# Three moves in a fused attention, mixing and FFN kernel: tile 2's weights, unit passes, the first block's centring

## The chip, the cores and the metric

The kernel runs on one core of one Trainium2 chip. The metric is the device time of one execution in microseconds (us); smaller is better. TensorE (PE) multiplies matrices into PSUM, VectorE (DVE), ScalarE (ACT) and GpSimd (POOL) work on tiles in SBUF, and SyncE (SP) issues most DMAs. Each engine runs its instructions in the order in which they are written; between engines there are semaphores. TensorE's clock has two levels here, 1.2 and 2.4 GHz; the profile gives the granted clock of a stretch as a share of the higher one.

## The reference

Three stages follow one another on 4 batches of 768 tokens with 384 channels. The first is a recurrent attention; the change leaves its arithmetic alone. Then:

```python
# mixing of tokens (x: [4, 768, 384])
theta = x @ w_theta
zr, zi = x * cos(theta), x * sin(theta)
y = einsum('ts,bsd->btd', w_tok_r, zr) + einsum('ts,bsd->btd', w_tok_i, zi)
u = x + y
x = u + max(u @ w_ch, 0)                 # "channel product"
# feed-forward network (FFN)
mu, var = mean(x), mean((x - mu) ** 2)   # over the channels
xn = (x - mu) / sqrt(var + 1e-6) * g_ln
out = x + max(xn @ w_ch1, 0) @ w_ch2     # 384 -> 1536 -> 384
```

All weights arrive as 64-bit numbers. Each product is made of three: a value is split into a rounded high part and the rest (names ending in h and l, or hi and lo), and high times high, low times high and high times low are added up in PSUM.

## The kernel before

**Attention** runs 24 chunks and takes about the first 229 us. `late(c, k)`, called in slot k of chunk c, puts the beginnings of the next stage into it.

**Mixing** is a loop over the 24 pairs of MIX: batch b and block s of 128 source tokens. The first 12 steps take blocks 0 to 2 of each batch, the rest blocks 3 to 5. Step i multiplies z of block i with the mixing weights of token tile s: `mix(i, 0)` and `mix(i, 1)`, 18 matmuls each. Between the halves come a channel product if one is due, then the angles of step i + 2: `theta` (9 matmuls of x with w_theta), `angles` (kk on ScalarE, nf on VectorE), `sines` and `cosines` (ScalarE), and the transposes and copies of x for the step after that (pt, xh, xl, u). At the start of step i, `turn(i + 1)` multiplies x with the sines and cosines (zf on VectorE) and rounds it (zh on ScalarE), and `rest(i + 1)` subtracts (zl on VectorE). So zl of a step is made while the step before it is multiplied. PSUM tiles pc, pth, pt and pst share two buffers under the tag "pa".

**Weights.** The class Weights handles the 64-bit weights in units, one behind the other in the order in which they were queued. A unit is loaded (raw; two staging buffers), its magnitude is taken (ScalarE, line 765; in attention's slots VectorE, line 761, and the clamps at once), it is clamped (VectorE, lines 771 and 772), assembled (VectorE, lines 781 and 782) into one of three buffers t, and split into hi (ScalarE, line 795) and lo (POOL or VectorE, line 802). `step()` does a piece of this in each late slot of attention. `pump()` does it in the loop: it finishes the unit before the last one, assembles the last one and begins the next. PA[i] pumps stand between turn and rest of step i; PB[i] pumps behind the angles, where only the clamps are done ahead of the channel product. The units are w_theta, the mixing weights w0 to w5 (w(s,q): tile s, half q), FFN weights that are multiplied with g on POOL and stored as 32-bit numbers in DRAM (`stash`, tile flat), and w_ch. At last the FFN weights f0 to f3 are loaded back from flat and split.

**The first FFN block's preparation** is the list of `pre(0)`: split of u, three channel products, the sum of u over the channels on VectorE (`total`), the mean subtracted and the rest split (`centre`: a product with ones into pst, then three rounds of subtraction, rounding and subtraction), the squares (ScalarE) and their sum (POOL, `total` again), and `rstd`: again a product with ones, then square root, reciprocal and one step of refinement on VectorE, ScalarE and POOL. The loop places these pieces in steps 15 to 23.

**FFN.** From 441.9 us on, 8 blocks of 12 features' tiles run on a TensorE that hardly pauses: `up` (9 matmuls into ph; hh on ScalarE, hl on VectorE), and two tiles later `down` (9 matmuls into acc).

The lines that the change touches move: line 795 becomes 797, 802 becomes 804, and from line 848 on six are added, so that zl's line 916 is 922 and the channel product's addition 992 is 998.

Of the kernel before, what the change touches and what calls it, by code (L numbers as in the profile page):

```python
# [7 lines left out]
F32R = mybir.dt.float32r  # L8
# [654 lines left out]
C = 384  # L663
# [9 lines left out]
class Weights:  # L673
# [110 lines left out]
    def parts(self, u, raw, t, clamped):  # L784
        nc = self.nc
        self.ready.add(u[0])
        if len(u) == 5:
            dst, g = u[3:]
            w = t[:, 0].rearrange("p (k c) -> p k c", k=KB)
            nc.gpsimd.tensor_tensor(out=w, in0=w, in1=bc(g.unsqueeze(2), [128, KB, 128]), op=ALU.mult)  # L790
            self.stores.append((dst, t))
            return lambda: None
        hi, lo, scale, split = u[3:]
        if scale is None:
            nc.scalar.copy(out=hi, in_=t)
            n = t.shape[1]
            split = n if split is None else split

            def low():
                for e, r in ((nc.gpsimd, slice(0, split)), (nc.vector, slice(split, n))):  # L800
                    if r.stop > r.start:
                        e.tensor_tensor(out=lo[:, r], in0=t[:, r], in1=hi[:, r].bitcast(F32), op=ALU.subtract)
        else:
            nc.scalar.activation(out=hi, in_=t, func=AF.Copy, scale=scale)

            def low():
                nc.vector.scalar_tensor_tensor(out=lo, in0=t, scalar=scale, in1=hi.bitcast(F32), op0=ALU.mult, op1=ALU.subtract)
        return low


class Mixer:
# [21 lines left out]
    def load_w(self, s, wtok, pool, wts, w=None):  # L833
        w = self.W[s] = w or [pool.tile([128, 4, C], F32R, name=f"w{s}_{i}") for i in range(2)]
        for q in range(2):
            wts.add(("w", s, q), wtok[s, q], w[0][:, 2 * q:2 * q + 2], w[1][:, 2 * q:2 * q + 2], split=0 if s > 1 else None)

# [265 lines left out]
def build(tc, a):  # L1103
# [8 lines left out]
    with tc.manual_schedule(), outer:  # L1112
# [14 lines left out]
        def late(c, k):  # L1127
# [11 lines left out]
            if (c, k) == (19, 2):  # L1139
                mx.open(ph1, tc)  # L1140
                for s in range(2):
                    mx.load_w(s, a["wtok"], mx.cst, wts)
                wts.load()
# [35 lines left out]
        for s in (2, 3, 4, 5):  # L1179
            mx.load_w(s, a["wtok"], None, wts, [slot(f"w{s}_{i}", 2 * (s - 2) + i, [128, 4, C], F32R) for i in range(2)])  # L1180
        spare = ExitStack()
# [11 lines left out]
        def two_f(f, hi, lo):  # L1193
            for n in range(2):
                ff.load_f(f + n, flat, hi[:, 2 * n:2 * n + 2], lo[:, 2 * n:2 * n + 2], wts)

        SLOTS = {"uh": 2, "ul": 3, "xh": 6, "xl": 7}
        soon = {"uh": 0, "ul": 1}
# [8 lines left out]
        n = len(MIX)  # L1207
        PA = [3] + [1] * 21 + [2] * 2
        PB = [0] * 18 + [1] * 4 + [2] * 2
        wp = Late()  # L1210
# [3 lines left out]
        for i in range(n):  # L1214
            b, s = MIX[i]
            assert ("w", s, 1) in wts.ready
            if i + 1 < n:
                mx.turn(i + 1)
            for _ in range(PA[i]):
                wts.pump()  # L1220
            if i + 1 < n:
                mx.rest(i + 1)
            mx.mix(i, 0, yp)
            for _ in range(PB[i]):
                wts.clamps()
            for k in {16: (1,), 17: (2,), 18: (3,)}.get(i, ()):
                todo[k]()
# [16 lines left out]
            if i == 7:  # L1244
                spare.close()
                ff.load_ch(a["wch"], outer.enter_context(tc.tile_pool(name="wch", bufs=1)), wts)
                stash(range(6, NF))
            if i == 17:
                two_f(0, *[slot(f"f0_{k}", k, [128, 4, C], F32R) for k in range(2)])
            if i == 22:  # L1250
                two_f(2, *[slot(f"f2_{k}", 4 + k, [128, 4, C], F32R) for k in range(2)])
            assert i < 15 or ("c", 2) in wts.ready, wts.todo
            if i == 15:
                wp.pool = ff.sp = Spare(mx.cst, ("w1_0", "w1_1"))
            for k in {15: (0,), 20: (4,), 21: (5,), 22: (6,), 23: (7,)}.get(i, ()):
                todo[k]()
# [64 lines left out]
```

## Time and profile before

| | us |
|---|---|
| median of 3 runs | 791.89 (790.45 to 794.86) |
| profiled execution, own time | 792.09 |
| span in the trace | 790.3 |
| TensorE busy | 709.3 (90%) |
| VectorE busy | 518.8 (66%) |
| ScalarE busy | 356.7 (45%) |
| POOL busy | 212.2 (27%) |
| mean granted TensorE clock | 0.968 |

Times in the rows below count from the start of the span. A row of the time-ordered view has the start, the duration, the engine, the line, what it writes and reads, and in brackets the engine's idle time just ahead of it with what ended that time.

### The profile page before, as it was taken

The page shows a single profiled execution, that of the slowest core. Times are in us where ns is not written, and L with a number is a line of the kernel's source. Part 1 is how long each engine was busy: PE and PEld are TensorE (multiplying, and loading weights), DVE is VectorE, ACT ScalarE, POOL GpSimd, SP SyncE. Part 2 cuts the span into 40 slices and gives each one's busy share as a digit, 9 for nine tenths or more (in the row PEclk, how much of TensorE's full clock was granted, in tenths as well). Part 3 has the DMA queues.
Part 4 walks back from the last instruction along what each step waited for, and adds up shares of the span by engine and source line. Part 5 has one row for each costly group of instructions (what it writes and reads, how often), then busy time and mean ns, then how long its engine had stood idle before and what let it go on. Part 6 is the DMA issues. An engine that isn't in the chain of part 4 may idle for free.

```text
span 790.3 us, 19137 instructions
## 1 busy us (share of the span) xinstructions
PE 709.3 (90%) x8059; PEld 654.2 (83%) x8062; DVE 518.8 (66%) x868; ACT 356.7 (45%) x782; POOL 212.2 (27%) x232
## 2 busy tenths in 40 slices
PE   4588788777686999999999899999999999999997
PEld 2455555544466999999999899999999999999997
DVE  5889989986858888889886555435353444444342
ACT  1267776787765776555444334122223222131210
POOL 4755655743110001202120332313121112112120
PEclk7799999999998999999999999999999999999999
DMA  8767766324434223542350130000000000000000
GB/s 265 232 178 209 196 194 185 117 89 133 155 134 170 80 76 105 148 133 80 120 179 22 60 100 1 31 1 31 1 31 1 30 1 31 1 1 31 1 31 30
DMA packets 29717, 71.41 MB, mean 90 GB/s; under 512 B 4928, under 2 KB 17472, under 8 KB 29632
## 3 DMA queue, kind: packets, MB, share of 16 engines
q1 hardware_dynamic: 29632, 70.19, 28.5%
q8 instruction: 63, 1.03, 0.6%
q14 instruction: 22, 0.18, 0.1%
HBM read 56.02 MB, written 9.44 MB: 83 GB/s over the span
## 4 chain that ended last, share of the span: by engine, by line
PE 68%; DVE 16%; ACT 7%; issue 3%; DMA 3%; POOL 2%; SPq 1%; ACTq 0%; DVEq 0%; POOLq 0%
PE acc L1068 19%; PE ph L1049 19%; PE y L935 14%; PE pc L990 4%; PE pth L875 3%; ACT bdw L439 3%; DVE prod L356 3%; PE S L447 2%; DVE XT L365 1%; PE py L473 1%; DMA raw<-wtok 1%; PE RW L435 1%; DVE t L781 1%; DVE u L944 1%; DVE Ti L365 1%
## 5 line engine op out<-in xcount | busy, mean ns | idle before, releaser
L935 PE MATMUL y<-w,zh 128*128 128x384 f32 x576 | 154.1, 341 | 1.8 <-ACT zh L910 1.3
L1068 PE MATMUL acc<-hh,f 128*128 128x384 f32 x576 | 147.2, 336 | 0.0
L1054 DVE SCALAR_TENSOR_TENSOR hl<-ph,hh 128x384 fp32r<-128x384 f32 x96 | 52.3, 553 | 112.7 <-ACT hh L1053 112.7
L1053 ACT ACTIVATE hh<-ph 128x384 fp32r<-128x384 f32 x96 | 46.7, 491 | 162.9 <-PE ph L1049 162.9
L1049 PE MATMUL ph<-xh,f 128*128 128x384 f32 x576 | 117.2, 338 | 0.0
L935 PEld LDWEIGHTS y<-w,zh 128*128 128x128 f32 x576 | 105.4, 189 | 2.4 <-ACT zh L910 1.6
L935 PE MATMUL y<-w,zl 128*128 128x384 f32 x288 | 98.3, 341 | 8.1 <-DVE zl L916 8.1
L1068 PEld LDWEIGHTS acc<-hh,f 128*128 128x128 f32 x576 | 104.5, 188 | 0.0
L1049 PEld LDWEIGHTS ph<-xh,f 128*128 128x128 f32 x576 | 102.8, 189 | 0.0
L1068 PE MATMUL acc<-hl,f 128*128 128x384 f32 x288 | 97.2, 337 | 2.4 <-DVE hl L1054 2.4
L1049 PE MATMUL ph<-xl,f 128*128 128x384 f32 x288 | 66.0, 337 | 0.0
L439 ACT COPY bdw<-RW 32x192 f32<-32x192 f32 x192 | 59.6, 310 | 10.7 <-PE RW L435 8.1
L935 PEld LDWEIGHTS y<-w,zl 128*128 128x128 f32 x288 | 55.0, 191 | 8.7 <-DVE zl L916 8.7
L1068 PEld LDWEIGHTS acc<-hl,f 128*128 128x128 f32 x288 | 54.2, 188 | 2.7 <-DVE hl L1054 2.7
L452 ACT COPY bds<-S 48x384 f32<-48x384 f32 x92 | 43.5, 473 | 28.3 <-PE S L447 26.9
L447 PE MATMUL S<-bdw,ktt 128*48 128x192 f32 x368 | 42.0, 352 | 15.3 <-ACT bdw L439 15.1
L790 POOL TENSOR_TENSOR t<-t,g 128x384 f32<-128x384 f32 x12 | 16.9, 1411 | 137.9 <-DVE t L782 134.8
L1049 PEld LDWEIGHTS ph<-xl,f 128*128 128x128 f32 x288 | 52.0, 189 | 0.0
L435 PEld LDWEIGHTS RW<-Rs,pt 32*32 32x32 f32 x1472 | 19.5, 108 | 31.8 <-DVE Rs L427 24.4
L447 PEld LDWEIGHTS S<-bdw,ktt 128*48 128x48 f32 x368 | 20.7, 128 | 29.9 <-ACT bdw L439 23.8
L1078 POOL TENSOR_TENSOR o<-u,o 128x384 f32<-128x384 f32 x21 | 20.8, 1017 | 85.0 <-DVE o L1077 85.0
L435 PE MATMUL RW<-Rs,pt 32*32 32x48 f32 x1472 | 25.8, 208 | 16.3 <-DVE Rs L427 16.2
(159 smaller groups left out, 1297.7 us busy)
## 6 DMA issues: line engine op xcount, KB each, us to landing
kqt<-kq SPq DMA_DIRECT2D x20, 512.0 KB, 5.9
raw<-wtok SPq DMA_DIRECT2D x12, 768.0 KB, 4.3
raw<-wff SPq DMA_DIRECT2D x12, 768.0 KB, 4.9
bdk<-kq SPq DMA_DIRECT2D x40, 192.0 KB, 4.2
vt<-vin SPq DMA_DIRECT2D x24, 192.0 KB, 4.8
ktt<-ktok SPq DMA_DIRECT2D x24, 192.0 KB, 4.0
x<-ys SPq DMA_DIRECT2D x96, 48.0 KB, 2.6
flat<-t SPq DMA_DIRECT2D x12, 384.0 KB, 5.5
```

Source lines behind the costliest of these rows:

```text
L356: eng.tensor_tensor(out=pr[:, j], in0=bc(lhs[:, j].unsqueeze(2), [128, i, c, kk]), in1=bc(rhs[:, j].unsqueeze(1), [128, i, c, kk]), op=ALU ...
L435: nc.tensor.matmul(RW[h][rr, 1, j, :], PT[c // 4][rr, m0 + j, :], Rs[rr, j, :], start=True, stop=True)
L439: nc.scalar.copy(out=b[rr, :, r, :], in_=RW[h][rr, 1, :, :])
L447: nc.tensor.matmul(S_ps[h][64 * e:64 * e + D, g, :], KT[c][:, 2 * h + g, e, :], b[:, 2 * g + e, :, :], start=(c == 0 and g == 0), stop=Tru ...
L452: nc.scalar.copy(out=n[ee, :, e, :], in_=S_ps[h][ee, :, :].rearrange("p g (r d) -> p (g r) d", r=4))
L875: nc.tensor.matmul(ps, l[:, k], self.tw[w][:, k], start=(n == 0), stop=(n == 8))
L935: nc.tensor.matmul(self.Y[q], l[:, ri, 128 * k:128 * k + 128], self.W[s][w][:, 2 * ri + h], start=(first and w == ri == 0 and l is zh), st ...
L990: nc.tensor.matmul(ps, self.wc[w][:, k, 128 * e:128 * e + 128], r[:, k], start=(n == 0), stop=(n == 8))
L1049: nc.tensor.matmul(ps, w[:, 0, 128 * k:128 * k + 128], r[:, k], start=(n == 0), stop=(n == 8))
L1053: nc.scalar.activation(out=hh, in_=ps, func=AF.Relu)
L1054: nc.vector.scalar_tensor_tensor(out=hl, in0=ps, scalar=0.0, in1=hh.bitcast(F32), op0=ALU.max, op1=ALU.subtract)
L1068: nc.tensor.matmul(self.ACC[j][e], w[:, 1, 128 * e:128 * e + 128], r, start=(f == 0 and n == 0), stop=(f == NF - 1 and n == 2))
```

## The change

1. `load_w` may be given its target tiles later, and the units of token tile 2 are queued together with those of tiles 0 and 1, in slot (19, 2) of attention. The DMA of w(2,0) is issued some 13 us earlier, and its magnitude and clamps are done by VectorE in attention's last slot; the DMA of w(2,1) goes ahead of the last chunk's stores of x.
2. In step 0, rest(1) stands straight behind turn(1), ahead of the pumps, which are two instead of three.
3. In steps 16 to 18 the pump moves from PA to PB, that is behind the channel product and the angles; steps 19 to 21 have their one pump in PA alone.
4. The sum of u is placed in step 18 (before: 20), the centring in 19 (21), the squares in 20 (22) and rstd in the middle of 22 (the end of 23). The centred tiles xh and xl take buffer slots 0 and 1 (before: 6 and 7).
5. f0 and f1 are queued in step 21 (before: 17), for slots 6 and 7.

```diff
@@ parts, load_w
+        if callable(hi):
+            hi, lo = hi(), lo()
...
     def load_w(self, s, wtok, pool, wts, w=None):
-        w = self.W[s] = w or [pool.tile([128, 4, C], F32R, name=f"w{s}_{i}") for i in range(2)]
+        if pool:
+            w = [pool.tile([128, 4, C], F32R, name=f"w{s}_{i}") for i in range(2)]
+        self.W[s] = w
         for q in range(2):
-            wts.add(("w", s, q), wtok[s, q], w[0][:, 2 * q:2 * q + 2], w[1][:, 2 * q:2 * q + 2], split=0 if s > 1 else None)
+            r = slice(2 * q, 2 * q + 2)
+            wts.add(("w", s, q), wtok[s, q], lambda r=r: self.W[s][0][:, r], lambda r=r: self.W[s][1][:, r],
+                    split=0 if s > 1 else None)
@@ late, slot (19, 2)
-                for s in range(2):
-                    mx.load_w(s, a["wtok"], mx.cst, wts)
+                for s in range(3):
+                    mx.load_w(s, a["wtok"], mx.cst if s < 2 else None, wts)
@@ before the loop
         for s in (2, 3, 4, 5):
...
+            if s > 2:
+                mx.load_w(s, a["wtok"], None, wts, w)
+            mx.W[s] = w
...
-        SLOTS = {"uh": 2, "ul": 3, "xh": 6, "xl": 7}
+        SLOTS = {"uh": 2, "ul": 3, "xh": 0, "xl": 1}
...
-        PA = [3] + [1] * 21 + [2] * 2
-        PB = [0] * 18 + [1] * 4 + [2] * 2
+        PA = [2] + [1] * 15 + [0] * 3 + [1] * 5
+        PB = [0] * 16 + [1] * 3 + [0] * 3 + [1] * 2
@@ the loop
             if i + 1 < n:
                 mx.turn(i + 1)
+            if i == 0:
+                mx.rest(1)
             for _ in range(PA[i]):
                 wts.pump()
-            if i + 1 < n:
+            if 0 < i < n - 1:
                 mx.rest(i + 1)
...
-            for k in {16: (1,), 17: (2,), 18: (3,)}.get(i, ()):
+            for k in {16: (1,), 17: (2,), 18: (3,), 22: (7,)}.get(i, ()):
...
-            if i == 17:
-                two_f(0, *[slot(f"f0_{k}", k, [128, 4, C], F32R) for k in range(2)])
+            if i == 21:
+                two_f(0, *[slot(f"f0_{k}", 6 + k, [128, 4, C], F32R) for k in range(2)])
...
-            for k in {15: (0,), 20: (4,), 21: (5,), 22: (6,), 23: (7,)}.get(i, ()):
+            for k in {15: (0,), 18: (4,), 19: (5,), 20: (6,)}.get(i, ()):
```

How the order of VectorE's instructions changes is seen at three places. A row has the source line, the operation, what it writes and reads, and the size; x_70 is the block of x that becomes z of step 1.

VectorE at the end of attention and in step 0, before:

```order
L861 TENSOR_TENSOR xl<-pt,xh 128x384
L909 TENSOR_TENSOR zf<-zf,x_70 128x768
L771 TENSOR_SCALAR t<-t 128x768
L772 TENSOR_SCALAR t<-t 128x768
L781 SCALAR_TENSOR_TENSOR t<-raw,t 128x768
L782 SCALAR_TENSOR_TENSOR t<-raw,t 128x768
L771 TENSOR_SCALAR t<-t 128x768
L772 TENSOR_SCALAR t<-t 128x768
L781 SCALAR_TENSOR_TENSOR t<-raw,t 128x768
L782 SCALAR_TENSOR_TENSOR t<-raw,t 128x768
L802 TENSOR_TENSOR w_1_4259<-t,w_0_4258 128x768
L916 TENSOR_TENSOR zl<-zf,zh 128x768
```

and after:

```order
L761 TENSOR_SCALAR t<-raw 128x768
L771 TENSOR_SCALAR t<-t 128x768
L772 TENSOR_SCALAR t<-t 128x768
L867 TENSOR_TENSOR xl<-pt,xh 128x384
L915 TENSOR_TENSOR zf<-zf,x_70 128x768
L922 TENSOR_TENSOR zl<-zf,zh 128x768
L781 SCALAR_TENSOR_TENSOR t<-raw,t 128x768
L782 SCALAR_TENSOR_TENSOR t<-raw,t 128x768
L771 TENSOR_SCALAR t<-t 128x768
L772 TENSOR_SCALAR t<-t 128x768
L781 SCALAR_TENSOR_TENSOR t<-raw,t 128x768
L782 SCALAR_TENSOR_TENSOR t<-raw,t 128x768
```

zl, which stood behind two whole units, now follows zf, and the magnitude and clamps of a unit have come to stand ahead of xl.

VectorE in steps 16 and 17, before; u_65 is the block that the channel products are added to:

```order
L909 TENSOR_TENSOR zf<-zf,x_2922 128x768
L771 TENSOR_SCALAR t<-t 128x768
L772 TENSOR_SCALAR t<-t 128x768
L781 SCALAR_TENSOR_TENSOR t<-raw,t 128x768
L782 SCALAR_TENSOR_TENSOR t<-raw,t 128x768
L916 TENSOR_TENSOR zl<-zf,zh 128x768
L992 SCALAR_TENSOR_TENSOR u_65<-pc,u_65 128x384
L885 SCALAR_TENSOR_TENSOR nf<-kk,pth 128x384
L865 TENSOR_TENSOR u_4250<-u_4250,pt 128x3x128
L861 TENSOR_TENSOR xl<-pt,xh 128x384
L909 TENSOR_TENSOR zf<-zf,x_72 128x768
```

and after:

```order
L915 TENSOR_TENSOR zf<-zf,x_2922 128x768
L922 TENSOR_TENSOR zl<-zf,zh 128x768
L771 TENSOR_SCALAR t<-t 128x768
L772 TENSOR_SCALAR t<-t 128x768
L998 SCALAR_TENSOR_TENSOR u_65<-pc,u_65 128x384
L891 SCALAR_TENSOR_TENSOR nf<-kk,pth 128x384
L871 TENSOR_TENSOR u_4258<-u_4258,pt 128x3x128
L867 TENSOR_TENSOR xl<-pt,xh 128x384
L781 SCALAR_TENSOR_TENSOR t<-raw,t 128x768
L782 SCALAR_TENSOR_TENSOR t<-raw,t 128x768
L915 TENSOR_TENSOR zf<-zf,x_72 128x768
```

Ahead of each addition into u_65 (line 992, now 998) stood four passes of a unit; now its two clamps stand there, and the other two passes come behind xl.

VectorE from step 22 to the FFN's first block, before; w_0 and w_1 in the rows of lines 1002 to 1036 hold the sums, f_1 is the low part of FFN weights:

```order
L909 TENSOR_TENSOR zf<-zf,x_72 128x768
L916 TENSOR_TENSOR zl<-zf,zh 128x768
L1002 TENSOR_TENSOR w_0_5626<-w_1_5627,w_0_5626 128x384
L944 TENSOR_TENSOR u_4251<-u_4251,y 128x384 x3
L802 TENSOR_TENSOR f_1_6211<-t,f_0_6210 128x384 x2
L944 TENSOR_TENSOR u_4251<-u_4251,y 128x384 x3
L1031 TENSOR_SCALAR w_1_5627<-pst 128x384
L1033 RECIPROCAL rs<-rs 128x384
L1034 SCALAR_TENSOR_TENSOR w_1_5627<-w_1_5627,rs 128x384
L1036 SCALAR_TENSOR_TENSOR rs<-w_1_5627,rs 128x384
L1054 SCALAR_TENSOR_TENSOR hl<-ph,hh 128x384 x3
```

and after, from step 21 on:

```order
L1008 TENSOR_TENSOR w_0_5626<-w_1_5627,w_0_5626 128x384
L915 TENSOR_TENSOR zf<-zf,x_2921 128x768
L922 TENSOR_TENSOR zl<-zf,zh 128x768
L891 SCALAR_TENSOR_TENSOR nf<-kk,pth 128x384
L915 TENSOR_TENSOR zf<-zf,x_72 128x768
L922 TENSOR_TENSOR zl<-zf,zh 128x768
L1037 TENSOR_SCALAR w_1_5627<-pst 128x384
L1039 RECIPROCAL rs<-rs 128x384
L1040 SCALAR_TENSOR_TENSOR w_1_5627<-w_1_5627,rs 128x384
L1042 SCALAR_TENSOR_TENSOR rs<-w_1_5627,rs 128x384
L804 TENSOR_TENSOR f_1_6164<-t,f_0_6163 128x384
L950 TENSOR_TENSOR u_4259<-u_4259,y 128x384 x3
```

The sum's subtraction (line 1002, now 1008) has come to stand ahead of zf and zl of steps 22 and 23, and the four rows of rstd (1031 to 1036, now 1037 to 1042) ahead of the subtractions for f0 to f3 instead of behind them.

## Rows read from the trace of the kernel before

**Rows 1.** The page's row of busy time, share and instructions, by engine.

```profile
PE 709.3 (90%) x8059; PEld 654.2 (83%) x8062; DVE 518.8 (66%) x868; ACT 356.7 (45%) x782; POOL 212.2 (27%) x232
```

**Rows 2.** PE's waits, 215 to 460 us: total, times, longest.

```profile
PE y L935 <- DVE zl L916: 8.1, 2, 7.5
...
PE pt L848 <- DVE u L992: 2.6, 2, 1.5
PE acc L1068 <- DVE hl L1054: 2.4, 1, 2.4
```

**Rows 3.** Stretches of 2 us: length, busy PE to POOL, PEclk, DMA share, GB/s.

```profile
434.00:436.00 2.00, 1.20 (x5) 0.95 (x6) 0.96 (x1) 1.26 (x2) 0.66 (x1) 1.00 0.00 0
...
450.00:452.00 2.00, 2.00 (x9) 2.00 (x8) 0.35 (x1) 0.00 (x0) 0.00 (x0) 0.59 0.95 316
452.00:454.00 2.00, 2.00 (x8) 2.00 (x8) 0.56 (x1) 0.83 (x1) 0.92 (x1) 0.55 0.72 267
```

**Rows 4.** Time-ordered, DVE's clamp beside POOL's subtraction; a later subtraction of POOL.

```profile
207.91 2.18 DVE L772 TENSOR_SCALAR t<-t 128x768 uint32<-128x768 uint32 x1
...
207.83 1.84 POOL L802 TENSOR_TENSOR w<-t,w 128x768 fp32r<-128x768 f32 x1 [20.19 <-ACT w L795]
...
228.33 1.85 POOL L802 TENSOR_TENSOR w<-t,w 128x768 fp32r<-128x768 f32 x1 [5.25 <-ACT w L795]
```

**Rows 5.** Start of mixing: two pieces of the chain that ended last, then DVE and PE.

```profile
231.80 4.65 DMA raw<-wtok
...
250.29 1.56 PE pth L875 x9
...
245.31 0.55 DVE L885 SCALAR_TENSOR_TENSOR nf<-kk,pth 128x384 f32<-128x384 f32 x1
...
252.30 0.95 DVE L916 TENSOR_TENSOR zl<-zf,zh 128x768 fp32r<-128x768 f32 x1
...
245.44 0.69 PE L935 MATMUL y<-w,zl 128*128 128x384 f32 x1 [7.54 <-DVE zl L916]
...
255.34 0.34 PE L935 MATMUL y<-w,zl 128*128 128x384 f32 x1
```

**Rows 6.** Time-ordered, step 16, DVE.

```profile
372.66 0.55 DVE L771 TENSOR_SCALAR t<-t 128x768 f32<-128x768 f32 x1
...
376.58 0.55 DVE L992 SCALAR_TENSOR_TENSOR u<-pc,u 128x384 f32<-128x384 f32 x1
```

**Rows 7.** Time-ordered, steps 19 to 23, ACT, DVE and PE.

```profile
402.29 0.92 ACT L765 ACTIVATE t<-raw 128x768 f32<-128x768 f32 x1 [1.27 <-DMA flat<-t]
...
408.36 0.53 ACT L892 ACTIVATE zf<-nf 128x384 f32<-128x384 f32 x1 [0.56 <-DVE nf L885]
...
434.10 1.16 ACT L1024 ACTIVATE uh<-ul 128x1152 f32<-128x1152 f32 x1
...
409.98 0.96 DVE L909 TENSOR_TENSOR zf<-zf,x 128x768 f32<-128x768 f32 x1 [0.72 <-ACT zf L900]
...
426.76 0.56 DVE L1017 SCALAR_TENSOR_TENSOR ul<-pst,u 128x384 f32<-128x384 f32 x1 [0.20 <-PE pst L1008]
...
432.30 0.95 DVE L909 TENSOR_TENSOR zf<-zf,x 128x768 f32<-128x768 f32 x1
...
438.03 0.56 DVE L1002 TENSOR_TENSOR w<-w,w 128x384 fp32r<-128x384 f32 x1 [2.84 <-ACT w L1001]
...
434.25 0.44 PE L935 MATMUL y<-w,zh 128*128 128x384 f32 x1 [1.28 <-ACT zh L910]
```

**Rows 8.** Time-ordered, start of the FFN, PE and ACT.

```profile
441.87 0.51 PE L1049 MATMUL ph<-xh,f 128*128 128x384 f32 x2
...
449.47 0.44 PE L1068 MATMUL acc<-hl,f 128*128 128x384 f32 x1 [2.41 <-DVE hl L1054]
...
455.50 0.33 PE L1049 MATMUL ph<-xh,f 128*128 128x384 f32 x1
...
452.17 0.83 ACT L795 CAST f<-t 128x768 fp32r<-128x768 f32 x1 [4.92 <-DMA t<-flat]
```

More of the change, by code (lines that the diff above doesn't have):

```diff
@@ L1179, in build @@
         for s in (2, 3, 4, 5):
-            mx.load_w(s, a["wtok"], None, wts, [slot(f"w{s}_{i}", 2 * (s - 2) + i, [128, 4, C], F32R) for i in range(2)])
+            w = [slot(f"w{s}_{i}", 2 * (s - 2) + i, [128, 4, C], F32R) for i in range(2)]
+            if s > 2:
+                mx.load_w(s, a["wtok"], None, wts, w)
+            mx.W[s] = w
         spare = ExitStack()
```

## The prediction

> **What bounds the kernel now.** The first view to read is the busy time per engine: TensorE (PE) works 709.3 of 790.3 us [rows 1], so from the first mixing step to the end only an idle or slow TensorE can be won back. The second is the list of what PE waited for between 215 and 460 us [rows 2]: 8.1 us for zl, nearly all of it in one wait, 2.6 us in two waits for the addition of a channel product into u, 2.4 us in one wait for hl, all on VectorE (DVE). Each lies where this change moves something. The third view is the granted clock: after the wait for hl, which ends at 449.47 [rows 8], it is 0.59 and then 0.55 for two stretches of 2 us [rows 3], so between its two levels, 1.2 and 2.4 GHz. That cost 2 x 0.41 + 2 x 0.45 = 1.7 us more. After two short waits at 434 us it stayed at 1.00 [rows 3, 7]. I take from this that a wait of about 2.4 us brings a price of 1.7 us on top and waits under 1.5 us bring none; between them nothing is shown. Then I went through the time-ordered rows of four places. Step n is the n-th pass of the mixing loop; zl(n) is what step n multiplies.
>
> **Place A, the start of mixing.** PE waits 7.54 us for zl(1) until 245.44 [rows 5]. zl(1) was computable by 234, but on DVE it is written behind the passes of two weight units, and these wait for a load issued only when attention ends (4.65 us at 231.80 [rows 5]). After the change zl(1) stands ahead of those passes, and the first unit of tile 2 arrives during attention. So this wait goes. What is late next? zl(2) still stands behind unit passes, and the next unit's load needs a staging buffer that DVE must first have read. I follow the chain. The clamps of the unit now stand ahead of xl on DVE, and they run into GpSimd's (POOL's) subtraction of 228.33 to 230.18 [rows 4]. Earlier the same clamp took 2.18 us instead of its usual 0.56 when it began beside such a subtraction, and it ended just after it [rows 4]. So I let the clamps end at 230.2. Then xl 0.5, zf 0.9, zh 0.9, zl(1) 0.95 and small gaps give 233.9; two passes of 0.9 free the buffer at 235.7; load 4.65, to 240.4; its magnitude on ScalarE (ACT) 0.9 and kk 0.56, to 241.9, where nf of step 2's row starts instead of at 245.31. From that nf to the end of zl(2) the rows show 252.30 + 0.95 - 245.31 = 7.94 us [rows 5], and the order in between is unchanged: zl(2) ends at 249.8. PE used it at 255.34 before [rows 5], now at 249.85: **5.5 us won**. PE meanwhile is there at about 247.7: from 245.44 - 7.54 = 237.9, when it was free for zl(1), one step of 8.15 (nine matmuls take 1.56 [rows 5], so the 45 of a step 7.8, and three transposes 0.35), 1.3 us waiting for a PSUM buffer of theta that nf(2) frees, and 0.35 for the products with zh. So a new wait of 2.1 us remains, close to the one that slowed the clock. I charge 1.7: **A = +3.8**. Bounds: +5.5 without the clock's fall; +2.5 if the tile's units come another microsecond later.
>
> A rule of the Trainium skill speaks against the added clamps. The row has shown 2.18 us beside POOL's subtraction. The page "SBUF — State Buffer", section "Terms", says that DVE and GpSimd lock a shared port pair for a whole instruction and the loser is fully blocked. The trace agrees in that the clamp ended with POOL's instruction. Without such blocking the chain would begin 0.9 us earlier and A would be about +4.7.
>
> **Place B, steps 16 to 18.** The addition u<-pc releases the PSUM buffer for which the transposes wait, twice: 1.5 us and so 1.1 us [rows 2], the shorter one in step 16, where u<-pc ends at 376.58 + 0.55 = 377.13 [rows 6]. Ahead of it on DVE stood four unit passes and zl: from 372.66 to 376.58 [rows 6]. Now only zl and two clamps stand there; the two long passes come behind the copies. u<-pc can then end at about 376.3, 0.8 us earlier, and the 1.5 us of the other step vanish, because u<-pc no longer waits for another unit's clamps ahead of it. **B = +2.3**. The two passes now lie ahead of the next zf, where DVE had idle time in the same step, so I cost them at nothing; if that cover fails, up to 1 us.
>
> **Place C, steps 19 to 22.** The centring moves from the end of step 21 to the end of step 19, the squares from 22 to 20, and one unit's passes stay in steps 19 to 21. What goes: PE's waits for zh and zl behind the centring, 1.28 at 434.25 and 0.55 after it [rows 2, 7], 1.8 us. What comes:
> First, the staging tile: a magnitude on ACT waited 1.27 us for a store to DRAM [rows 7]; the store now leaves about 5 us later. Between 0 and 1.3 us of PE's time; I take 0.5, since most of ACT's delay falls in time in which it would have been idle.
> Second, zl(21). Behind the centring's start DVE has the centring, 426.76 to 432.30 = 5.5 us [rows 7], then zf 0.9, the four passes and zl 3.9 [rows 6]: 10.4 us with a small gap, beginning 0.5 us after step 19's last product. PE wants zl(21) 0.35 + 8.15 = 8.5 us after it. Wait 10.9 - 8.5 = 2.4 us. Bounds: 0, if the passes find room ahead of the centring; 4, if their unit comes late.
> Third, zl(22). From zl(21), 2.4 us into step 21, DVE has three additions and nf (1.9), ACT the sines 408.36 to 409.98 = 1.6 [rows 7], then squares, POOL's sums, cast and subtraction 434.10 to 438.59 = 4.5 [rows 7], all now ahead of zf(22); then zf 0.9, zh 0.9, zl 0.95. That is 13.2 us after step 20's end, and PE comes there after 2.4 + 7.9 + 0.1 = 10.4: wait 2.8 us. This chain doesn't depend on PE, so if the clock falls after the first wait, the second is shorter by as much; a fall costs nothing here unless it comes after the second (1.7).
> **C = 1.8 - 0.5 - 2.4 - 2.8 = -3.9**, between +1.8 and -6.9.
>
> **Place D, the FFN's start.** hl of the first feature block stood on DVE behind the rstd chain, so PE waited 2.41 us at 449.47 and then ran slow [rows 3, 8]. From PE's first product at 441.87 to the fifth up-projection at 455.50 are 13.6 us [rows 8]. The work is six groups of 9 matmuls at 1.56 [rows 5], 9.4 us. rstd now lies in the middle of step 22, its table load on ACT too, under PE's products. **D = +4.2** if nothing else is late. What else could be: f0 to f3 are now converted only from step 22 on, and f3's load needs the staging tile that f0's subtraction frees, which stands behind rstd on DVE. I have f0 done at 440.6 and f3's load landed at 443.7, its subtraction at 445.6, where PE wants it at 446.4: 0.8 us of slack. The longest landing of such a load here made ACT wait 4.92 us [rows 8]; with it D would be 2.5 us less, and 1.7 if the clock falls.
>
> **The sum** against the profiled execution's own 792.1 us (span 790.3 and 1.8 around it; the median of the runs, 791.9, is 0.2 below): 3.8 + 2.3 - 3.9 + 4.2 = 6.4, so **785.7 us**. Moved DMA issues on SyncE's queue cost nothing by themselves: w2's raw load goes ahead of attention's last four x stores, and each issue there takes some 0.6 us of a queue that no engine waits for until mixing starts.
>
> **The rivals.**
> 1. Less waiting than I charge: the clock holds in A (+1.7) and the passes find room around the centring, so that one of C's two waits goes (+2.4). For it: DVE is busy 66% of the span. Against it: the order on DVE is fixed, and the rows fill it in steps 19 to 21. About 782 to 783.
> 2. VectorE becomes the bound in steps 19 to 22: the clock falls after the second wait too (1.7), or the first wait is 4 instead of 2.4 us because the unit comes late (1.6), and f3 is late by its longest landing (2.5): 785.7 + 1.7 + 2.5 = 789.9; without f3, 787.3. For it: 10.4 us of work in a window of 8.5.
> 3. Slower: the first FFN products wait for f3. If the v sums reach rstd no earlier than before, it ends on DVE at 448.9 as before, f0's subtraction follows at 449.8, f3 lands 4.9 later, cast and subtraction take 1.8: 456.5 where PE wants f3 at 448.1 in that frame. That is 8.4 us of wait and 1.7 of clock on top: 785.7 + 10.1 = 795.8. It makes the kernel slower from an f3 that is 5.5 us later than I put it: 0.8 of slack, 4.7 of wait and 1.7 of clock eat the 6.4. Against it: the whole chain would have to slip by most of a step.
> 4. The change does nothing: zl(2) inherits the wait of zl(1) in full and C eats the rest. The chain at A would have to come 5 us later, for which I see no row. Within 0.5% of 791.9.
>
> **How the numbers follow.** 0.5% (4 us, to 787.9 or 795.8) is about what a measurement of this kernel can tell from no change. Forecast, 783.5 to 787.5: 0.43. Rival 1: 0.24. Rival 2: 0.20, half of it under 787.9 us. Rival 3: 0.06, rival 4: 0.07. Faster 0.43 + 0.24 + 0.10 = 0.77, of which I move 0.05 to same, because four places with errors of a microsecond or two each stand behind the sum: 0.72; same 0.22; slower 0.06. The range runs from rival 1 with a short C (781.5) to rival 2's end (790.0).
>
> **What would show it.** A: the waits list without the 7.5 us, a wait for zl near 249 of 2 to 3 us, the clock at 0.5 to 0.6 behind it. B: no wait of the transposes for u near 377 and 398 us. C: two waits for zl or zh near 417 to 435 of 2 to 3 us each. D: no wait for hl, 9.4 us from the first product to the fifth up-projection. Wrong at A if PE waits over 4 us for zl(2); wrong at D if up-projections wait for f2 or f3.

## The result

The changed kernel takes 786.07 us (median of seven executions, six of them between 784.49 and 788.52), the kernel before 791.89. The ratio is 0.9909, 95% interval 0.9881 to 0.9938: 0.9% faster, about 7 us by the ratio and 5.8 by the medians. Forecast were 785.7 us. One of the seven took 3205 us, with matmuls 2.7 to 4 times as long throughout (those of `mix` 1380 ns instead of 342); the trace of the changed kernel used here is therefore from a second series (785.81 us median, ratio 0.9903, interval 0.9873 to 0.9934), from an execution of 785.19 us with a span of 783.1.

The page of the changed kernel, busy time and instructions by engine [rows 1], and then what TensorE waited for between 228 and 462 us: in total, how often, the longest [rows 2].

```profile
PE 708.3 (90%) x8062; PEld 652.3 (83%) x8062; DVE 520.0 (66%) x869; ACT 354.2 (45%) x781; POOL 211.0 (27%) x232
```

```profile
PE y L941 <- DVE u L950: 2.4, 1, 2.4
PE y L941 <- DVE zl L922: 2.3, 2, 1.9
PE pst L1014 <- DVE nf L891: 1.2, 1, 1.2
PE pth L881 <- DVE nf L891: 1.1, 1, 1.1
...
PE ph L1055 <- DVE u L950: 0.4, 1, 0.4
PE pt L854 <- DVE u L998: 0.2, 1, 0.2
```

TensorE's work is the same to 0.2%. The 7.5 us for zl(1), the 1.3 us for zh and the 2.4 us for hl have gone, and of the 2.6 us for u 0.2 are left; six new waits (the row for zl holds two), 7.4 us in all, have come.

To see where the time went I use TensorE's own rows as marks, since they come in the same order in every kernel up to step 18: the first product of theta in step 0, in step 8 and in step 19, and the first and the fifth up-projection. First three marks of the kernel before (the other two are in [rows 8]), then five of the changed kernel.

```profile
232.55 0.68 PE L875 MATMUL pth<-tw,xh 128*128 128x384 f32 x3
...
307.27 1.03 PE L875 MATMUL pth<-tw,xh 128*128 128x384 f32 x5
...
405.09 1.20 PE L875 MATMUL pth<-tw,xh 128*128 128x384 f32 x6
```

```profile
232.72 0.50 PE L881 MATMUL pth<-tw,xh 128*128 128x384 f32 x2
...
302.31 1.03 PE L881 MATMUL pth<-tw,xh 128*128 128x384 f32 x5
...
397.63 0.68 PE L881 MATMUL pth<-tw,xh 128*128 128x384 f32 x3
...
438.84 0.41 PE L1055 MATMUL ph<-xh,f 128*128 128x384 f32 x1 [0.44 <-DVE u L950]
...
448.29 1.04 PE L1055 MATMUL ph<-xh,f 128*128 128x384 f32 x5
```

| stretch | before, us | after, us | won | forecast |
|---|---|---|---|---|
| A: step 0 to step 8 | 74.72 | 69.59 | +5.1 | +3.8 |
| B: step 8 to step 19 | 97.82 | 95.32 | +2.5 | +2.3 |
| C: step 19 to the first up-projection | 36.78 | 41.21 | -4.4 | -3.9 |
| D: first to fifth up-projection | 13.63 | 9.45 | +4.2 | +4.2 |
| sum | | | +7.4 | +6.4 |

Each column is one trace. Attention ended 0.2 us later in that of the changed kernel, which makes the 7.2 us between the two spans.

### The profile page after: what moved, and what is told of

It is laid out like the page before. It is cut to its first block, busy times and chain, and to the rows that moved or that the text cites. A ratio compares the mean times of both kernels' runs of the same rounds, so it can differ in the third digit from the quotient of the medians.

```text
span 3202.9 us, 19132 instructions
## 1 busy us (share of the span) xinstructions
PE 3183.2 (99%) x8059; PEld 2373.5 (74%) x8062; DVE 520.9 (16%) x869; ACT 360.2 (11%) x781; POOL 202.6 (6%) x232
## 4 chain that ended last, share of the span: by engine, by line
PE 99%; DVE 0%; issue 0%; ACT 0%
PE y L941 27%; PE ph L1055 18%; PE acc L1074 18%; PE pth L881 7%; PE S L447 6%; PE pc L996 5%; PE pa L174 3%; PE RW L435 3%; PE RW L424 3%; PE py L473 3%; PE py L462 3%; PE pt L854 1%; PE py L525 1%; PE pst L1014 1%; PE pa L225 0%
## 5 line engine op out<-in xcount | busy, mean ns | idle before, releaser
L941 PE MATMUL y<-w,zh 128*128 128x384 f32 x576 | 696.4, 1380 | 0.0
L941 PEld LDWEIGHTS y<-w,zh 128*128 128x128 f32 x576 | 525.5, 915 | 48.9 <-issue 48.4
L1074 PE MATMUL acc<-hh,f 128*128 128x384 f32 x576 | 472.0, 964 | 0.0
L1055 PE MATMUL ph<-xh,f 128*128 128x384 f32 x576 | 423.2, 979 | 0.0
L941 PE MATMUL y<-w,zl 128*128 128x384 f32 x288 | 392.8, 1364 | 0.0
L1055 PEld LDWEIGHTS ph<-xh,f 128*128 128x128 f32 x576 | 295.1, 513 | 100.4 <-issue 83.2
L1074 PEld LDWEIGHTS acc<-hh,f 128*128 128x128 f32 x576 | 286.5, 498 | 101.7 <-issue 83.9
L941 PEld LDWEIGHTS y<-w,zl 128*128 128x128 f32 x288 | 263.4, 914 | 22.5 <-issue 22.2
L1074 PE MATMUL acc<-hl,f 128*128 128x384 f32 x288 | 277.3, 963 | 0.0
L1055 PE MATMUL ph<-xl,f 128*128 128x384 f32 x288 | 225.2, 974 | 0.0
```

Of the source, the lines that this page charges most:

```text
L941: nc.tensor.matmul(self.Y[q], l[:, ri, 128 * k:128 * k + 128], self.W[s][w][:, 2 * ri + h], start=(first and w == ri == 0 and l is zh), st ...
L1055: nc.tensor.matmul(ps, w[:, 0, 128 * k:128 * k + 128], r[:, k], start=(n == 0), stop=(n == 8))
L1074: nc.tensor.matmul(self.ACC[j][e], w[:, 1, 128 * e:128 * e + 128], r, start=(f == 0 and n == 0), stop=(f == NF - 1 and n == 2))
```

## The experiments

Times are medians. Ratios are to the kernel before, run on the same chip at the same time; that kernel's median was 794.25 us beside the first four kernels, 793.40 beside the next four, 792.82 and 793.68 beside the last two pairs. Where a trace is compared with another, it is by the marks above. The first run is the changed kernel itself.

> The changed kernel once more, for a trace in which TensorE runs at its usual pace. By the prediction: 784.5 to 787.5 us; the 7.5 us wait for zl(1) gone and one of 2 to 3 us for zl(2) in its place; no waits of the transposes for u near 377 and 398 us; two waits for zl or zh of 2 to 3 us in steps 21 and 22; 9.4 us from the FFN's first product to its fifth up-projection. By the rival that the waits in steps 21 and 22 don't arise and something of A, B or D fell short by as much: waits under 1 us there, and a wait in one of the other three places.

Measured: 785.81 us, ratio 0.9903. The waits are in the list above. For place B the list holds 0.2 us; for D the marks give 9.45 us. Of the two waits of 2 to 3 us in steps 21 and 22 one came, put down to u; the other is 0.39 us. Places A and C follow below.

**Each place alone, on the kernel before.** Place A:

```diff
+                for s in range(3):            # slot (19, 2): tile 2 queued with 0 and 1
+                    mx.load_w(s, a["wtok"], mx.cst if s < 2 else None, wts)
+            if i == 0:
+                mx.rest(1)                    # ahead of the pumps
-        PA = [3] + [1] * 21 + [2] * 2
+        PA = [2] + [1] * 21 + [2] * 2
```

> Place A alone, on the kernel before: the units of token tile 2 queued in attention's slot (19, 2), rest(1) ahead of the pumps of step 0, two pumps there. Theory: 3.8 us faster (788.1 us), as zl(2) waits 2.1 us and the clock falls behind it; 5.5 us faster (786.4) if the clock holds. Rival, that the wait is only inherited by zl(2): within 1 us of the kernel before, with a wait for zl(2) of 6 us or more.

Measured: 788.34 us, ratio 0.9934 (0.9911 to 0.9956), 5.2 us faster by the ratio (3.5 to 7.1 by its interval). From step 0 to step 18 the trace has 157.61 us where before had 162.69: 5.1 us. The two waits that stay, theta's 0.50 for nf and 1.89 for zl(2), are those of the theory, and the inherited wait of 6 us is not there. The clock fell to 0.50 behind zl(2), for which the theory had 3.8 us; by the trace it is 1.3 more. The interval of the medians doesn't tell 3.8 from 5.5.

Place B:

```diff
-        PA = [3] + [1] * 21 + [2] * 2
-        PB = [0] * 18 + [1] * 4 + [2] * 2
+        PA = [3] + [1] * 15 + [0] * 3 + [1] * 3 + [2] * 2
+        PB = [0] * 16 + [1] * 6 + [2] * 2
```

> Place B alone, on the kernel before: in steps 16 to 18 the one pump stands behind the channel product and the angles. Theory: 2.3 us faster (789.6 us), no wait of the transposes for u. Rival, that the passes only wait elsewhere: the wait for u gone and waits for zl or nf of 2 us in all in steps 17 to 19, time within 1 us of before.

Measured: 795.97 us, ratio 1.0026 (1.0002 to 1.0049): slower by about 2 us. Neither expectation held. The wait for u went as forecast: from step 8 to 19 the trace is 95.11 us long, 2.7 less than before. But from step 19 to the fifth up-projection it is 54.93 us, 4.5 more. The row that costs it is in step 22; first ScalarE's and VectorE's, then TensorE's:

```profile
425.94 0.83 ACT L795 CAST f<-t 128x768 fp32r<-128x768 f32 x1
...
426.80 0.56 DVE L802 TENSOR_TENSOR f<-t,f 128x384 fp32r<-128x384 f32 x1 [1.71 <-ACT f L795]
427.28 1.75 DVE L916 TENSOR_TENSOR zl<-zf,zh 128x768 fp32r<-128x768 f32 x1
...
429.08 0.69 PE L935 MATMUL y<-w,zl 128*128 128x384 f32 x1 [2.55 <-DVE zl L916]
```

The clock at 0.67 and 0.50 behind this wait costs some 1.3 us more by TensorE's busy time. Step 18 has one pump fewer in this kernel, every later unit comes one pump later, and the conversion of an FFN weight falls between zf and zl, right ahead of the centring. In the changed kernel f0 and f1 are queued in step 21 only, and nothing of them lies there. So place B seems to pay only together with that part of the change; this is read from the rows, and no run has place B with f0's later place alone.

Places C and D:

```diff
-        SLOTS = {"uh": 2, "ul": 3, "xh": 6, "xl": 7}
+        SLOTS = {"uh": 2, "ul": 3, "xh": 0, "xl": 1}
+        PA = [3] + [1] * 23
+        PB = [0] * 22 + [1] * 2
-            if i == 17:                       # f0, f1 -> slots 0, 1
+            if i == 21:                       # f0, f1 -> slots 6, 7
-            for k in {15: (0,), 20: (4,), 21: (5,), 22: (6,), 23: (7,)}.get(i, ()):
+            for k in {15: (0,), 18: (4,), 19: (5,), 20: (6,)}.get(i, ()):   # rstd: middle of step 22
```

> Places C and D alone, on the kernel before: the sum of u, the centring and the squares two steps earlier, rstd in the middle of step 22, f0 and f1 queued in step 21, pumps of steps 18 to 23 as in the changed kernel in number. Theory: 4.2 us won at the FFN's start, 3.9 lost to waits for zl(21) (2.4) and zl(22) (2.8), so 791.6 us, within 1 us of before. Rival 1 (the waits do not arise): 3 to 5 us faster, 787 to 789. Rival 3 (f3 late): slower than before, with waits of up-projections for f2 or f3.

Measured: 791.66 us, ratio 0.9970 (0.9949 to 0.9992), 2.4 us faster than the kernel beside it, so not within 1 us; that 791.6 us had been expected is chance, as the kernel beside it ran at 794.25. By the marks D wins 4.19 us (its stretch runs from 440.88 to 450.32), and the steps from 19 to there lose 2.8. Another 1.7 us come from step 18, where the second pump, whose clamps made the transposes wait 1.5 us [rows 2], is no longer there; that belongs to place B's sum. The theory's amount for D stands. C's is smaller and made up otherwise: the wait for the staging tile does not occur in this kernel, step 21 waits 2.16 us with the clock at 0.50 behind it, and zl(22) makes PE wait 0.30 us instead of 2.8.

**Place A taken apart.** First the units early, but rest(1) behind the pumps:

```diff
-            if i == 0:
-                mx.rest(1)
-            if 0 < i < n - 1:
+            if i + 1 < n:
                 mx.rest(i + 1)
```

> The changed kernel with rest(1) back behind the pumps of step 0; the units of tile 2 stay in attention. Theory: zl(1) ends near 239.8 instead of 234, PE waits some 2 us for it, but zl(2) ends at 249.5 as before, so PE only waits earlier instead of later: within 0.7 us of the changed kernel if the clock holds, up to 1.7 slower if it falls. Rival (rest(1) is what removed the 7.5 us): 4 us or more slower than the changed kernel.

Measured: 785.20 us, ratio 0.9913. The trace takes 69.46 us from step 0 to step 8, the changed kernel 69.59. PE now waits 2.33 us for zl(1), and no wait of theta or for zl(2) is listed, instead of 1.1 for nf and 1.9 for zl(2). The clock fell to 0.50 behind the 2.33 us, and the way to step 8 was no longer for it. With the units early, rest(1)'s new place is worth nothing.

Then rest(1) ahead, with tile 2's units in their old place:

```diff
-                for s in range(3):
-                    mx.load_w(s, a["wtok"], mx.cst if s < 2 else None, wts)
+                for s in range(2):
+                    mx.load_w(s, a["wtok"], mx.cst, wts)
-        PA = [2] + ...
+        PA = [3] + ...
```

> The changed kernel with tile 2's units back in their old place (queued after attention, three pumps in step 0); rest(1) stays ahead of the pumps. Theory: zl(1) needs no wait, but zl(2) ends near 252.4 instead of 249.5, as its unit's load is issued at 231.8 again: PE waits 4 to 5 us for zl(2), 2 to 3 us slower than the changed kernel, and up to 1.7 more with the clock. Rival (early loading brings nothing, the order on VectorE does): within 0.7 us of the changed kernel.

Measured: 791.98 us, ratio 0.9987 (0.9954 to 1.0020). In its trace theta waits 4.0 us for nf, and the way to step 8 is 72.43 us, 2.8 longer than the changed kernel's, as the theory has it, though the wait is theta's and zl(2) holds PE up by 0.28 us only. The median is 6.8 us above that of the kernel beside it, more than the theory's 2 to 3 and 1.7.

```profile
249.78 1.65 PE L881 MATMUL pth<-tw,xh 128*128 128x384 f32 x6 [4.04 <-DVE nf L891]
```

So the same kernel ran again:

> rest(1) alone ahead, tile 2's units in the old place, a second time, since its first trace was 2.9 us slower than the trace with the units early, from the first mixing step to the FFN, and the medians differed by 6.8 us. If the trace is right: 2.5 to 4 us slower than the changed kernel (788.3 to 789.8). If the medians were: 6 us or more slower (792), so little or no gain on the kernel before.

Measured: 789.93 us, ratio 0.9956 (0.9937 to 0.9975), 4.8 us above the kernel of the third buffer beside it (below) and 4.1 above the changed kernel's median; its trace has 72.26 us to step 8. Two traces agree on 2.7 to 2.8 us, the medians give 4 to 7. By the marks to step 8 (74.72 us before) the early units alone win 5.3 us, rest(1) ahead alone 2.3 to 2.5, both together 5.1: the two do not add up, and the early units do all of A's work. Why these medians lie further off than the traces stays open.

What sets the wait that is left at A? In the changed kernel the first unit of tile 3 loads only when VectorE has read the first of tile 2. One more staging buffer exists from attention's end on; here the unit gets it:

```diff
-            extra = self.more is not None and self.count % 3 == 0
+            extra = self.more is not None and self.count % 3 == 2
```

> The changed kernel with the first unit of tile 3 loaded into the extra staging buffer that exists from attention's end on, so that its load no longer waits for VectorE to have read the first unit of tile 2 (which unit gets that buffer is shifted by one). Theory (this buffer sets the wait that is left at place A): the load leaves near the end of attention's stores, nf(2) starts 1.8 us earlier, behind VectorE's own passes; the wait of theta for nf (1.1 us) goes, that for zl(2) falls from 1.9 to 1.2 or less: 1.8 us faster than the changed kernel (784.0 of 785.8). Rival (VectorE's passes, not the load, set it): within 0.5 us, with the same two waits.

Measured: 785.15 us, ratio 0.9897 (0.9881 to 0.9913). The trace is 67.30 us long from step 0 to step 8, 2.3 less than the changed kernel; theta no longer waits, and zl(2) makes PE wait 0.98 us. The mechanism is shown by the two waits and by the load, which leaves at 232.81 us, 1.0 ahead of the first theta, instead of at 235.85, 3.1 behind it. In the medians the gain is 0.7 us, within the interval of the changed kernel, so a faster version is not shown by this.

```profile
240.32 0.55 DVE L891 SCALAR_TENSOR_TENSOR nf<-kk,pth 128x384 f32<-128x384 f32 x1
...
248.32 0.44 PE L941 MATMUL y<-w,zl 128*128 128x384 f32 x1 [0.98 <-DVE zl L922]
```

**Place C taken apart**, on the changed kernel. Step 20's pump behind the angles:

```diff
-        PA = [2] + [1] * 15 + [0] * 3 + [1] * 5
-        PB = [0] * 16 + [1] * 3 + [0] * 3 + [1] * 2
+        PA = [2] + [1] * 15 + [0] * 3 + [1, 0, 1, 1, 1]
+        PB = [0] * 16 + [1] * 3 + [0, 1, 0, 1, 1]
```

> The changed kernel with step 20's pump behind the angles instead of ahead of rest(21). Theory (the passes hold up zl(21), but zl(22) hangs on a chain of its own): PE's wait of 2.4 us at the start of step 21 falls to 0.2 and the clock stays at 1.00, but zl(22), whose chain runs nf, sines, squares, sums, zf, zh, zl on VectorE, ScalarE and POOL, comes only 1 us earlier, so PE waits about 3.2 us for it in step 22 instead of 0.4: within 1.5 us of the changed kernel (784.3 to 786.5). Rival (the passes alone are the cause): 4 us faster than the changed kernel, 781.8, with no new wait over 0.5 us.

Measured: 786.57 us, ratio 0.9918 (0.9890 to 0.9946). The waits: 0.44 us for u at the start of step 21 (2.4 in the changed kernel), then 0.70 for u inside it and 1.21 for zh and 0.55 for zl in step 22. From step 20's theta to the first up-projection 30.37 us, in the changed kernel 31.30. The theory holds: one wait is traded for others. Its 3.2 us for zl(22) was too much (1.21 and 0.55).

The last part of the squares' sum behind zl(22):

```diff
         def total(src, key, defer=False):
...
+            def rest():                       # rounding on ScalarE, subtraction on VectorE
...
+            if not defer:
+                rest()
@@ the loop, behind rest(i + 1)
+            if i == 21:
+                todo[8]()                     # rest() of the squares' sum
```

> The changed kernel with the last part of the squares' sum (ScalarE's rounding and VectorE's subtraction) behind zl(22) instead of ahead of zf(22). Theory: the 2.4 us wait in step 21 and the clock's fall stay, only the 0.4 us wait for zl(22) goes: within 0.7 us of the changed kernel (785.1 to 786.3). Rival (this chain is what step 21 and 22 lose): 3 us or more faster.

Measured: 785.32 us, ratio 0.9899 (0.9873 to 0.9925). The 2.36 us wait stays, the wait for zl(22) goes, a wait of the first up-projection for u grows from 0.44 to 1.04 us; 29.62 us over the same stretch, 1.7 less than the changed kernel, by the trace, and 0.5 by the medians. By the trace this chain is worth more than the 0.4 us of the theory and less than the rival's 3. The clock did not fall in this trace, against the expectation; in the changed kernel's order a fall makes no difference to this stretch (see place C below).

Both:

> Both edits together. Theory: the two waits are in series, each hidden by the other, so only both together pay: 4.2 us faster than the changed kernel (2.4 wait, 1.65 clock, 0.4 wait), 781.6, no wait over 0.5 us between 410 and 436 us. Rival: something else ends last there, the pst wait of 1.2 us or f0 to f3, and it is within 2 us of the changed kernel.

Measured: 786.11 us, ratio 0.9916 (0.9887 to 0.9946); 29.57 us over the stretch, as with the second edit alone. The expectation of 4.2 us fell; the rival's 2 us hold, but it is neither of the two things that the rival named. What is late next are VectorE's additions into u, which free the PSUM buffers of y: 0.37 and 0.69 us in step 21, 0.55 for zl in 22, 1.04 ahead of the first up-projection. By the medians no edit at C is told from the changed kernel.

**Place D undone**, on the changed kernel, rstd back at the end of step 23:

```diff
-            for k in {16: (1,), 17: (2,), 18: (3,), 22: (7,)}.get(i, ()):
+            for k in {16: (1,), 17: (2,), 18: (3,)}.get(i, ()):
-            for k in {15: (0,), 18: (4,), 19: (5,), 20: (6,)}.get(i, ()):
+            for k in {15: (0,), 18: (4,), 19: (5,), 20: (6,), 23: (7,)}.get(i, ()):
```

> The changed kernel with rstd back at the end of step 23. Theory: 4.2 us slower than the changed kernel (790.0): hl waits behind rstd on VectorE, 2.4 us of wait and 1.7 of clock. Rival (f0 to f3 behind the square root and rstd are worth more, as f3 needs the staging tile of f0): 8 us or more slower, with a wait of an up-projection for f2 or f3. Rival (rstd's place is hidden anyway): under 1 us.

Measured: 792.01 us, ratio 0.9978 (0.9954 to 1.0001), 6 us slower than the changed kernel. From the first to the fifth up-projection its trace has 14.35 us, 4.9 more than the changed kernel: 3.1 us of wait, and some 1.5 by the clock at 0.71, 0.50 and 0.93 behind it. The size is near the theory's 4.2, but the wait is not the one it named; hl makes nothing wait:

```profile
442.87 0.99 POOL L1041 TENSOR_TENSOR w<-w,rs 128x384 f32<-128x384 f32 x1 [10.56 <-DVE w L1040]
...
443.81 2.27 POOL L804 TENSOR_TENSOR f<-t,f 128x384 fp32r<-128x384 f32 x2
...
444.86 1.33 PE L1055 MATMUL ph<-xh,f 128*128 128x384 f32 x3 [3.11 <-POOL f L804]
```

POOL does one step of rstd and then the subtractions for f0 to f3, in this order. With f0 queued in step 21, rstd's place decides when the up-projections have their weights. This is the mechanism of the prediction's third rival, at a smaller price than the 10.1 us written there. Another 1.2 us of this trace come from step 19, ahead of anything that this edit moved. There ScalarE waits 4.3 us for a store to DRAM (2.46 in the changed kernel), and PE after it:

```profile
403.76 0.91 PE L1014 MATMUL pst<-w,ones 128*128 128x384 f32 x2 [3.03 <-DVE nf L891]
```

## Why the prediction was right, and where it was not

**Place A, right as to the chain.** The prediction had the clamps end at 230.2 us, zl(1) at 233.9, the load land at 240.4, nf start at 241.9, zl(2) end at 249.8 and its first product start at 249.85. The time-ordered rows of the changed kernel, VectorE, ScalarE, then TensorE [rows 4, 5]:

```profile
228.56 2.15 DVE L772 TENSOR_SCALAR t<-t 128x768 uint32<-128x768 uint32 x1
...
233.00 0.96 DVE L922 TENSOR_TENSOR zl<-zf,zh 128x768 fp32r<-128x768 f32 x1 [0.96 <-ACT zh L916]
...
241.47 0.55 DVE L891 SCALAR_TENSOR_TENSOR nf<-kk,pth 128x384 f32<-128x384 f32 x1 [1.73 <-ACT kk L890]
...
248.50 0.95 DVE L922 TENSOR_TENSOR zl<-zf,zh 128x768 fp32r<-128x768 f32 x1
...
240.09 0.89 ACT L765 ACTIVATE t<-raw 128x768 f32<-128x768 f32 x1 [3.35 <-DMA raw<-wtok]
...
242.18 1.28 PE L881 MATMUL pth<-tw,xh 128*128 128x384 f32 x6 [1.14 <-DVE nf L891]
...
249.51 0.44 PE L941 MATMUL y<-w,zl 128*128 128x384 f32 x1 [1.89 <-DVE zl L922]
```

None is off by more than 0.6 us, because every piece had a duration from a row and only the order was new. The two waits, put at 1.3 and 2.1 us, are 1.14 and 1.89. The clamp took 2.15 us until 230.71, beside POOL's subtraction of 228.47 to 230.30. The Trainium skill, page "SBUF — State Buffer", section "Terms", lets the loser of the shared port pair wait for the whole instruction; both this row and [rows 4] agree. In the traces of A alone and of both edits at C the clamp began 0.2 us ahead of POOL's subtraction (228.38 and 228.62; 233.88 and 234.11) and took 0.56 us. nf(2) then started 8.1 and 8.0 us behind the first mark instead of 8.75, 0.6 to 0.7 earlier where the prediction had 0.9. Step 8 did not come earlier (69.76 and 69.66 us against 69.59; the clock fell in both), so no trace shows that this wait of the clamp costs place A anything.

**Place A, wrong as to the clock.** The term that was mis-sized is the 1.7 us for a fall of the clock behind the wait for zl(2). It was wrong twice. First, the length of the wait for zl(2) does not decide it: behind 1.88 to 1.89 us the clock stayed at 1.00 in this trace, in those of the sum behind and of rstd late, and fell to 0.50 in those of A alone, of the pump behind and of both edits. Theta's wait ahead of it was 1.0 to 1.1 us in the first three and 0.4 to 0.7 in the others, so it is not the longer idle time that went with a fall; what decides is not shown. Second, where it fell it cost little by step 8: 69.66, 69.76 and 69.96 us in the three traces with a fall, 69.40, 69.48 and 69.59 in those without. The kernel with both edits at C equals the changed kernel at A; its stretches of 2 us behind the wait (columns as in [rows 3], TensorE's busy time alone):

```profile
252.00:254.00 2.00, 0.69 (x4) 1.00 0.20 34
254.00:256.00 2.00, 1.43 (x6) 0.76 0.85 335
256.00:258.00 2.00, 2.00 (x8) 0.50 0.07 29
258.00:260.00 2.00, 2.00 (x12) 0.89 0.00 0
```

and its first theta and that of step 8:

```profile
238.51 0.68 PE L881 MATMUL pth<-tw,xh 128*128 128x384 f32 x3
...
308.17 1.03 PE L881 MATMUL pth<-tw,xh 128*128 128x384 f32 x5
```

69.66 us, against 69.59 in the changed kernel's trace. The changed kernel, faster behind the wait, ran into VectorE in steps 3 to 8. There zl ends, and its first product follows at once:

```profile
297.56 1.58 DVE L922 TENSOR_TENSOR zl<-zf,zh 128x768 fp32r<-128x768 f32 x1
...
299.20 0.44 PE L941 MATMUL y<-w,zl 128*128 128x384 f32 x1
```

whereas in the trace with the fall the same zl lies ready for 1.0 us (it ends at 304.21, the product starts at 305.23):

```profile
302.63 1.58 DVE L922 TENSOR_TENSOR zl<-zf,zh 128x768 fp32r<-128x768 f32 x1
...
305.23 0.34 PE L941 MATMUL y<-w,zl 128*128 128x384 f32 x1
```

So the gain at A was 5.8 us at the product of zl(2) (255.34 to 249.51), close to the forecast without the charge (5.5), and 5.1 by step 8, where VectorE's pace has the last word. The prediction had used this very argument at place C and not at A. What it did not name is that the kernel before also ran slowly behind its wait, at 0.54 to 0.75 from 242 to 250 us:

```profile
246.00:248.00 2.00, 2.00 (x8) 0.50 0.64 264
```

By TensorE's busy time this cost some 1.8 us, and the steps up to 8, some 8.15 us each, did not give it back. That it went is part of the gain, beside 4.5 us of shorter waits (7.54 to 1.14 and 1.89).

**Place B, right**: 2.5 us for 2.3. That the move costs time without f0's later place was not foreseen.

**Place C, right in its sum, with its terms shifted.** The changed kernel's rows [rows 7], ScalarE, VectorE, then TensorE:

```profile
401.96 0.90 ACT L765 ACTIVATE t<-raw 128x768 f32<-128x768 f32 x1 [2.46 <-DMA flat<-t]
...
413.57 0.95 DVE L922 TENSOR_TENSOR zl<-zf,zh 128x768 fp32r<-128x768 f32 x1
414.44 1.47 DVE L950 TENSOR_TENSOR u<-u,y 128x384 f32<-128x384 f32 x3
...
403.97 0.62 PE L1014 MATMUL pst<-w,ones 128*128 128x384 f32 x2 [1.16 <-DVE nf L891]
...
415.14 0.66 PE L941 MATMUL y<-w,zh 128*128 128x384 f32 x1 [2.37 <-DVE u L950]
...
425.30 0.44 PE L941 MATMUL y<-w,zl 128*128 128x384 f32 x1 [0.39 <-DVE zl L922]
```

The wait that comes from the store was put at 0.5 and is 1.16 us; the bound of 1.3 held here, but not in the trace of rstd late (3.03). The wait in step 21 was put at 2.4 and is 2.37, though the last to arrive is not zl(21) but the addition into u behind it, which frees a PSUM buffer for step 21's sums; the prediction had not looked at that buffer. The wait for zl(22) was put at 2.8 and is 0.39 here. The reason given for a fall that costs nothing is what took its place: the clock was 0.74, 0.50 and 0.91 in the three stretches from 414 us on, and PE came later to zl(22). In the trace of rest(1) alone the clock did not fall behind the same wait. The clock of the two traces, the changed kernel's first, then rows of the second:

```profile
416.00:418.00 2.00, 2.00 (x8) 0.50 0.00 0
...
422.00:424.00 2.00, 1.42 (x8) 1.00 0.00 0
```

```profile
422.58 0.41 PE L941 MATMUL y<-w,zh 128*128 128x384 f32 x1 [2.36 <-DVE u L950]
...
431.76 0.44 PE L941 MATMUL y<-w,zh 128*128 128x384 f32 x1 [1.08 <-ACT zh L916]
432.75 0.44 PE L941 MATMUL y<-w,zl 128*128 128x384 f32 x1 [0.56 <-DVE zl L922]
```

There PE waits 1.6 us in step 22, and from step 20's theta to the first up-projection both traces take 31.30 us (407.54 to 438.84, and 414.98 to 446.28). So do two more with a fall (units alone early, third buffer), and the second of rest(1) alone, without one, takes 31.29. With or without the fall the stretch is as long as VectorE and ScalarE make it. The 2.8 us was still 1.2 too much. That the up-projections would start behind the last additions into u (0.44 us) was missing. The lower bound of -6.9 does not come out of its own terms: 1.8 - 1.3 - 4 - 2.8 = -6.3.

**Place D, right**: 9.45 us as forecast, no wait for hl nor for f0 to f3 in the changed kernel. The slack of f3 held. The 2.5 us set against its longest load do not follow from the prediction's own times: 4.9 us instead of 3.1 would pass the slack of 0.8 by 1.0.

**The sum, partly luck.** By the marks 7.4 us were won, 1.0 more than the 6.4 of the sum: 1.3 more at A, 0.5 less at C. In C the 1.2 us too much for zl(22) were made up for by waits put too low or left out (0.7 more for the store, 0.44 for u). That the median of 786.07 lies 0.4 us from the forecast says little, as the median of the kernel before lies between 791.89 and 794.25 in five series.

**The rivals.** None came out, though one half of the first, the clock that holds at A, is what the changed kernel's trace shows. The second, VectorE as the bound of steps 19 to 22, is true as a description and was priced in the forecast already. The third shows itself as soon as rstd is put back.

## What to carry to other kernels

Follow the new order row by row with the old durations: a chain of ten known pieces was right to 0.6 us, while the one price set by rule, that of the clock, was wrong. Before charging or crediting anything on the bounding engine, ask how much slack the engine that feeds it has over the next steps, since a loss within that slack is given back and a gain beyond it is not kept. When parts of a change move a stream of staged work, try them together: one part alone was 2 us slower here and worth 2.5 us in company.

## What the runs showed that was not expected

The same 2.4 us wait at the start of step 21 was followed by a fall of the granted clock to 0.50 in the changed kernel's trace and in those with the units alone early and with the third buffer, and by none in those of the sum behind and of rest(1) alone (both times): how long TensorE waits does not settle it, and what does is not shown.

The end of attention moves between executions by more than the change is worth: the first theta of step 0 starts between 230.74 us (C and D alone) and 238.51 us (both edits at C) in the thirteen traces, though attention's arithmetic is the same in all. In the eight of them whose attention is written as in the changed kernel it lies between 230.80 and 238.51. In stretches of 10 us ahead of it the granted clock differs; from 205 us on, C and D alone, then the pump behind:

```profile
205.00:215.00 10.00, 6.83 (x179) 1.00 0.35 103
```

```profile
205.00:215.00 10.00, 7.70 (x112) 0.66 0.66 238
```

From the first theta on, the two traces of rest(1) alone agree within 0.2 us to step 8 and to the fifth up-projection. For a change behind attention the marks of one trace tell more than several medians, though one trace can be off too (the 3.0 us behind the store in that of rstd late), and where the two disagree, as for rest(1) alone (2.7 us and 4 to 7), the difference has not been explained.
